# Turning fifteen of sixteen x tiles by transposing loads, and moving the points at which two sets of weights are waited for

## The chip, the core and the metric

The kernel runs on one core of a Trainium2 chip. A core has engines with an instruction queue each: TensorE (PE in the profile; its weight loads are PEld), VectorE (DVE), ScalarE (ACT), GpSimd (POOL) and SyncE (SP), which here issues nearly all DMAs. Each engine runs its instructions in the order of its queue and waits on semaphores. Matrix products go from the on-chip memory (SBUF) into eight banks of a second one (PSUM), from which ScalarE and VectorE evacuate them. The metric is the time on the device in microseconds (us), as a median of several runs.

## The reference, cut to what matters

x has 2048 rows (tokens) of 1024. Two branches are computed from it and mixed by a gate:

```python
g = sigmoid((x * gate_w).sum(-1, keepdims=True))
# a: attention, 32 heads of 32, each token over 8 keys at distances 0, 2, .. 14
qkv = x @ wqkv                       # 1024 x 3072
a = softmax(q . k * scale) v @ wo    # over those 8 keys
# b: a gated MLP whose gate mixes tokens
z = gelu(x @ w_in)                   # 1024 x 3584, halves z1 and z2
z2 = layernorm(z2)
b = (z1 * (w_sp @ z2 + b_sp)) @ w_out
return g * a + (1 - g) * b
```

All inputs and the output are bf16.

## The kernel before

Everything is computed from x transposed. The tile `xT` holds it with the 1024 features on the partitions (8 blocks of 128) and the 2048 tokens along the row. Sixteen tiles of 128 tokens make up x.

**How x is turned.** There are two ways. Tiles 0 to 3 are loaded as they are into `xn` (lines 173 to 177) and turned by TensorE: `xpose` (L221) does eight 128x128 transposes into PSUM, and ScalarE (L228) and VectorE (L230) copy every other one into `xT`. Tiles 4 to 15 are loaded by a DMA that transposes (L179, DMA_TRANSPOSE in the profile) and need nothing else. `first_dma` and `chained` tie these first DMAs to each other, so that SP issues them in the order in which they are written; all later DMAs of SP stand behind them.

**The first products.** `keep_warm` issues matmuls on zeros. A small transpose (L324) and a copy (L325) put the gate's weights into a column of `wvp`, the weights of the first three head groups' v. `vp_tile(i)` (L299) multiplies x tile i with them, eight matmuls of 385 columns; in the first four of these the transposes of the next tile are put between the matmuls (`middle`). Then come q and k of head group 0 (`qk_tile`, L290, eight matmuls of 512 columns each, for 512 tokens), more v tiles, and so on. Products q.k are taken in blocks along the diagonal (`band_blocks`, L338; TensorE L356, evacuated by ScalarE at L364), stored to DRAM (`band_d`) and loaded back as `att_L` in a layout with one token's eight keys side by side. SP issues those stores and loads too.

**The attention on VectorE.** There are eight head groups of four heads. Of each, VectorE takes the maxima and subtracts them (L671 to L674), ScalarE takes the exponential (L662), VectorE sums and normalizes (L683 to L687, L692), multiplies with v (L708, four operations of 128x2048 for each half of a group) and adds up the products (L712, L713, L717).

**Products by Strassen's scheme.** Most large products are done as quads: a 2x2 block product by seven instead of eight block products (`strassen` L438, `chain` L499; the matmuls are at L435). In `chain` a quad has seven steps of four matmuls. After the first, ScalarE copies a bank as the seed of another (L518), after the second it copies a bank to SBUF (L524), and after the third and the fifth VectorE adds that copy to a bank (`plus`, L506). TensorE can go on into a bank only once its reader is done. Two quads run interleaved, step by step. The sums of weights that a quad needs are made by VectorE, four operations (`sums4_steps`, L577).

**What sets the order.** Engines run what is written in the order of writing, and a planner decides while the kernel is being written where VectorE's and ScalarE's side work goes. It keeps a clock for each engine; `advance` (L764) looks at what is due by the time of TensorE's clock (DMAs in `due`, the attention's streams, and a list `fill` of weight sums with the time from which each may be placed) and writes the earliest. Times in it are assumed ones. For the weights of the first z2 product, `load_later` (L988) registers eight loads and, when the planner holds the last for landed at time t, enters the four sums with t + `LATE`, 0.5 us:

```python
        def landed(t):
            land[0] += 1
            if land[0] == KT:
                fill.extend((t + LATE, 1.05, f) for f in wz_sums(p))
```

**The z1 stage.** Seven passes fp = 0 .. 6 (L1200) compute two quads each (`z1_quad`); ScalarE evacuates by gelu (L1168), and each quad's result is stored to DRAM (`store`, `z_d` in the profile). The weights of pass 0 are loaded alone and the others for two passes at a time, in two halves f, into `w1_pairs` (`load_w1`, L841). Those of passes 5 and 6 go where those of passes 1 and 2 were. They are loaded at the end of pass 2. In passes 2 to 4 eight transposing loads of w_sp (`load_raw`, L1109, 512 KB each) are put at given steps (`RAW_AT`, L1199), all on SP.

After these follow the token mixing (from L1577 on, by `strassen`) and the output product (L1468 and others), which the change does not touch.

## Time and profile before

| | |
|---|---|
| median of 9 runs | 655.79 us (654.79 to 657.12) |
| the profiled execution | 657.12 us |
| its span, from the first to the last instruction | 655.3 us |
| busy: TensorE, VectorE, ScalarE | 646.1, 518.6, 299.0 us |
| granted clock of TensorE, mean | 0.997 |
| transposing loads of x: SP busy with one (min / median / max) | 1.307 / 1.308 / 2.339 us |
| the same, issue to landing (min / median / max) | 3.7 / 3.9 / 4.9 us |
| matmuls 128x512 of bf16 in L294, mean | 380 ns (they overlap; one starts each 0.22 us) |

How to read it: times are those of one execution, counted from its first instruction. A row of a timeline has the start, the time from the start of its first to the end of its last instruction, the engine (with a q where it is its sequencer, which waits or issues), the line of the kernel, the operation, what it writes and reads, and how many are merged; in brackets stand the idle time before it and what ended it. A row of the waits has the waiting instruction, what released it, the total, the number and the longest. The granted clock is the share of its full clock that TensorE was given.

### The profile page before, as it was taken

The page shows a single profiled execution, that of the slowest core. Times are in us where ns is not written, and L with a number is a line of the kernel's source. Part 1 is how long each engine was busy: PE and PEld are TensorE (multiplying, and loading weights), DVE is VectorE, ACT ScalarE, POOL GpSimd, SP SyncE. Part 2 cuts the span into 40 slices and gives each one's busy share as a digit, 9 for nine tenths or more (in the row PEclk, how much of TensorE's full clock was granted, in tenths as well). Part 3 has the DMA queues.
Part 4 walks back from the last instruction along what each step waited for, and adds up shares of the span by engine and source line. Part 5 has one row for each costly group of instructions (what it writes and reads, how often), then busy time and mean ns, then how long its engine had stood idle before and what let it go on. Part 6 is the DMA issues. An engine that isn't in the chain of part 4 may idle for free.

```text
span 655.3 us, 11411 instructions
## 1 busy us (share of the span) xinstructions
PE 646.1 (99%) x4425; PEld 339.0 (52%) x4425; DVE 518.6 (79%) x820; ACT 299.0 (46%) x652; POOL 6.2 (1%) x15
## 2 busy tenths in 40 slices
PE   8999999999989999999999999999999999999998
PEld 4544467544445555444444444444444444868684
DVE  2533989999799999999898676977559999596862
ACT  4545677776676787899654112112121112202020
POOL 1000000000000000001000000000000000000000
PEclk9999999999999999999999999999999999999999
DMA  9989555696767104246994578559587375454501
GB/s 219 190 216 233 103 111 150 148 236 160 176 182 209 24 1 125 65 129 186 287 234 152 133 166 176 145 144 279 134 186 173 98 142 100 110 148 107 135 28 54
DMA packets 230198, 98.19 MB, mean 150 GB/s; under 512 B 177520, under 2 KB 217088, under 8 KB 230144
## 3 DMA queue, kind: packets, MB, share of 16 engines
q1 hardware_dynamic: 229856, 97.27, 61.0%
q8 instruction: 34, 0.56, 0.4%
q10 hardware_dynamic: 288, 0.20, 0.1%
q14 instruction: 20, 0.16, 0.1%
HBM read 45.10 MB, written 36.61 MB: 125 GB/s over the span
## 4 chain that ended last, share of the span: by engine, by line
PE 86%; DVE 5%; ACT 4%; DMA 3%; issue 1%; SPq 0%; DVEq 0%; ACTq 0%
PE psum_all L435 67%; PE psum_all L1468 8%; PE psum_all L294 7%; PE psum_all L304 3%; DMA arena<-in_B_w_in_dram 2%; ACT arena L870 1%; DVE arena L708 1%; PE psum_all L356 1%; ACT arena L1168 1%; DVE arena L577 1%; DVE psum_all L506 1%; DMA arena<-in_A_x_dram 1%; DVE arena L712 1%; ACT arena L815 0%; ACT arena L364 0%
## 5 line engine op out<-in xcount | busy, mean ns | idle before, releaser
L435 PE MATMUL psum_all<-arena 128*128 128x512 f16 (+6 forms) x2462 | 494.6, 363 | 3.5 <-DVE psum_all L506 2.4
L435 PEld LDWEIGHTS <-arena 128*128 128x128 f16 (+1 forms) x2462 | 240.1, 98 | 250.5 <-issue 7.2
L708 DVE TENSOR_TENSOR arena<-arena,att_A 128x2048 f16<-128x2048 bf16 x64 | 75.3, 1220 | 0.3
L294 PE MATMUL psum_all<-arena 128*128 128x512 bf16 x256 | 57.5, 380 | 0.0
L506 DVE TENSOR_TENSOR psum_all<-psum_all,arena 128x512 f32<-128x512 f32 (+1 forms) x74 | 48.5, 669 | 8.5 <-PE psum_all L435 4.7
L1468 PE MATMUL psum_all<-arena 128*128 128x256 f16 (+1 forms) x468 | 51.6, 273 | 0.0
L1468 PEld LDWEIGHTS <-arena 128*128 128x128 f16 x468 | 45.8, 98 | 5.5
L815 ACT ACTIVATE arena<-psum_all 128x448 bf16<-128x448 f32 x64 | 34.3, 544 | 20.3 <-PE psum_all L435 9.7
L453 ACT COPY psum_all<-psum_all 128x512 f32<-128x512 f32 (+1 forms) x24 | 12.5, 519 | 67.6 <-PE psum_all L435 66.8
L1168 ACT ACTIVATE arena<-psum_all 128x512 bf16<-128x512 f32 x56 | 31.2, 613 | 20.9 <-PE psum_all L435 8.7
L294 PEld LDWEIGHTS <-arena 128*128 128x128 bf16 x256 | 24.4, 98 | 28.4 <-issue 0.2
L712 DVE TENSOR_TENSOR arena<-arena 128x2048 f16<-128x2048 f16 x32 | 38.1, 1219 | 0.0
L364 ACT CAST arena<-psum_all 128x1988 f16<-128x1988 f32 (+3 forms) x25 | 34.0, 1359 | 2.7 <-PE psum_all L356 2.4
L870 ACT ACTIVATE arena<-arena 128x896 bf16<-128x896 bf16 x32 | 30.9, 979 | 0.0
L577 DVE TENSOR_TENSOR arena<-arena 128x512 f16<-128x512 bf16 (+3 forms) x52 | 25.5, 522 | 6.5 <-DMA arena<-in_B_w_in_dram 6.0
L297 ACT CAST arena<-psum_all 128x512 bf16<-128x512 f32 x32 | 18.6, 585 | 25.8 <-PE psum_all L294 25.8
L477 ACT COPY psum_all<-psum_all 128x512 f32<-128x512 f32 (+1 forms) x24 | 12.4, 518 | 37.5 <-PE psum_all L435 36.8
L581 DVE TENSOR_TENSOR arena<-arena 128x1024 f16<-128x1024 f16 (+2 forms) x17 | 12.2, 722 | 19.1 <-PE psum_all L435 15.7
L464 ACT COPY psum_all<-psum_all 128x512 f32<-128x512 f32 (+1 forms) x24 | 12.4, 517 | 25.8 <-PE psum_all L435 24.8
L459 ACT COPY arena<-psum_all 128x512 f32<-128x512 f32 (+1 forms) x24 | 12.7, 533 | 24.7 <-PE psum_all L435 22.5
L518 ACT COPY psum_all<-psum_all 128x512 f32<-128x512 f32 (+1 forms) x37 | 20.6, 567 | 5.7 <-PE psum_all L435 5.1
L304 PE MATMUL psum_all<-arena 128*128 128x385 bf16 x128 | 22.6, 327 | 0.0
(112 smaller groups left out, 522.3 us busy)
## 6 DMA issues: line engine op xcount, KB each, us to landing
arena<-v_d SPq DMA_DIRECT2D x8, 960.0 KB, 6.5
z_d<-arena SPq DMA_DIRECT2D x14, 512.0 KB, 4.5
arena<-z_d SPq DMA_DIRECT2D x14, 512.0 KB, 4.2
zg_d<-arena SPq DMA_DIRECT2D x56, 128.0 KB, 2.2
arena<-zg_d SPq DMA_DIRECT2D x32, 224.0 KB, 3.3
band_d<-arena SPq DMA_DIRECT2D x28, 248.5 KB, 4.0
arena<-in_A_wqkv_dram SPq DMA_DIRECT2D x16, 256.0 KB, 4.5
o_d<-arena SPq DMA_DIRECT2D x4, 1024.0 KB, 6.1
```

Of the source, the lines that this page charges most:

```text
L294: nc.tensor.matmul(ps[:], w[:, t, kt, :], xT[:, kt, 512 * c:512 * (c + 1)], start=(kt == 0), stop=(kt == KT - 1))
L304: nc.tensor.matmul(ps[:, 0:VP + 1], xT[:, kt, i * P:(i + 1) * P], wvp[:, kt, :], start=(kt == 0), stop=(kt == KT - 1))
L364: nc.scalar.copy(dst, src)
L435: nc.tensor.matmul(bank[:, 0:N], lhsT, rhs, start=(start and m == 0), stop=(m == n - 1), skip_group_check=True)
L506: last_add[0] = nc.vector.tensor_tensor(out[:, n], a[:, n], vs, ALU.add)
L577: return [lambda a=a: nc.vector.tensor_tensor(*a) for a in args]
L708: lambda ws=ws, in0=in0, in1=in1: tt(p5[:, ws], in0[:, ws], in1[:, ws], ALU.mult)), False
L712: lambda a=p3[:, ws], b=p3[:, ws.start + 4:ws.stop + 4]: tt(a, a, b, ALU.add)), not n
L815: nc.scalar.activation(z2[:, i + 8 * a, ZC * c:ZC * (c + 1)], bank[:, 0:ZC], ACT.Gelu_apprx_tanh, accum_out=s1[:, 4 * n + c:4 * n + c + 1])
L870: return nc.scalar.activation(junk, src, ACT.Square, accum_out=(s2, s2h)[x][:, n:n + 1])
L1168: last_gelu[0] = nc.scalar.activation(z1s[:, f, a, :], bank[:], ACT.Gelu_apprx_tanh)
L1468: nc.tensor.matmul(bank[:, h], l, r, start=(start and m == 0), stop=(m == len(ab) - 1), skip_group_check=True)
```

## The change

The diff has four parts.

1. Only x tile 0 is loaded plainly and turned by TensorE. Tiles 1 to 15 are loaded by transposing DMAs. The two loads of group 0's q and k weights stand behind tile 3 in SP's order (before: behind tile 5).
2. Two of the eight warm-up matmuls go, the transposes of tile 0 come ahead of the gate column's transpose, and nothing is put between the matmuls of the first v tiles.
3. The planner's allowance after the last z2 weight load is 4.0 instead of 0.5 us, so the four sums are written later.
4. In pass 2 of the z1 stage the third w_sp transpose moves to pass 3, the first half of the weights of passes 5 and 6 is loaded at step 6 of the pass, the second half at its end, and the two stores of pass 2 are issued behind both.

```diff
@@ -165,6 +165,7 @@
         for t in range(2):
             dma(wqk_slots[g][:, t], wq_v[:, :, t * D + g * C:t * D + (g + 1) * C])
 
+    PLAIN = 1
     nc.scalar.dma_start(gw_s[:], gw_v)
     def load_wvp(k, dma):
         dma(wvp[:, k:k + 2, 0:VP], wq_v[:, k:k + 2, 2 * D:2 * D + VP])
@@ -173,11 +174,9 @@
     first_dma(xn[:, 0:1, :], x_v[:, 0:1, :])
     for k in range(2, KT, 2):
         load_wvp(k, first_dma)
-    for i in range(1, 4):
-        first_dma(xn[:, i:i + 1, :], x_v[:, i:i + 1, :])
-    for i in range(4, 16):
+    for i in range(PLAIN, 16):
         chained(nc.sync.dma_start_transpose(xT[:, :, i * P:(i + 1) * P], x2[i * P:(i + 1) * P, :]))
-        if i == 5:
+        if i == 3:
             load_wqk(0, first_dma)
     load_wqk(1, first_dma)
     first_dma(bass.AP(tensor=v_d.tensor, offset=v_d.offset, ap=[[C, 16], [(S + 16) * C, NG], [1, C]]), zeros)
@@ -320,13 +319,13 @@
             pinned.setdefault(inst.ins.engine, inst.ins.name)
 
     keep_warm(6)
+    xpose(0)
     gwT = banks[1][:, 0:KT // 2].bitcast(BF)
     nc.tensor.transpose(gwT, gw_s[:], ident[0:KT, 0:KT])
     nc.vector.tensor_copy(wvp[:, :, VP:VP + 1], gwT.rearrange("p (k o) -> p k o", o=1))
-    keep_warm(2)
-    xpose(0)
+    pass
     for i in range(4):
-        vp_tile(i, middle=lambda: xpose(i + 1) if i < 3 else None)
+        vp_tile(i, middle=None)
     band_at = [0]
     last_sub = [None]
     last_evac = [None]
@@ -639,7 +638,7 @@
         sync.dma_start(v_t, bass.AP(tensor=v_d.tensor, offset=v_d.offset + (g * (S + 16) + 2) * C, ap=[[NJ * C, P], [1, NJJ * C]]))
 
 
-    FR, LATE = 0.4, 0.5
+    FR, LATE, WZ_LATE = 0.4, 0.5, 4.0
     t_bands, t_v = [FAR] * NG, [FAR] * NG
     sub_end, exp_end = [FAR] * NG, [FAR] * NG
     v_data = [0.0]
@@ -838,8 +837,8 @@
     def w1_half(fp, f):
         return w1_first[:, f] if fp == 0 else w1_pairs[(fp - 1) // 2 % 2][f][:, :, (fp - 1) % 2 * P:((fp - 1) % 2 + 1) * P]
 
-    def load_w1(fp):
-        for f in range(2):
+    def load_w1(fp, halves=(0, 1)):
+        for f in halves:
             to = w1_first[:, f] if fp == 0 else w1_pairs[(fp - 1) // 2 % 2][f]
             sync.dma_start(to, win_v[:, :, HF * f + fp * P:HF * f + (fp + (2 if fp else 1)) * P])
 
@@ -991,7 +990,7 @@
         def landed(t):
             land[0] += 1
             if land[0] == KT:
-                fill.extend((t + LATE, 1.05, f) for f in wz_sums(p))
+                fill.extend((t + WZ_LATE, 1.05, f) for f in wz_sums(p))
         for n, f in enumerate(load_wz(p)):
             dma(at + gap * n, 0.65, f, landed, True)
 
@@ -1141,7 +1140,7 @@
     z1s_slots = [[free(o + 2048 * r, 2048).rearrange("p (f a t) -> p f a t", f=2, a=2) for r in range(2)] for o in (T1_OFF, R_OFF + 16384)]
     zv_slots = [free(R_OFF + 20480 + 1024 * r, 1024, F32) for r in range(2)]
 
-    w1_left = [0]
+    w1_left, kept_stores = [0], []
 
     def w1_sums(fp):
         def one(f):
@@ -1167,7 +1166,10 @@
             act(0.6 + table("gelu"), max(clock["PE"], clock["DVE"] if f + a == 2 else 0.0) + 0.2)
             last_gelu[0] = nc.scalar.activation(z1s[:, f, a, :], bank[:], ACT.Gelu_apprx_tanh)
 
-        def store():
+        def store(now=False):
+            if fp == 2 and not now:
+                kept_stores.append(store)
+                return
             dst = z1_d[c].rearrange("p (f t) -> p f t", f=NF)[:, fp:fp + NFH + 1:NFH, :]
             last_store[0] = sync.dma_start(dst, z1s.rearrange("p f a t -> p f (a t)"))
 
@@ -1196,7 +1198,7 @@
     dma(clock["PE"] + 1.0, 2.9, lambda: load_w1(1), w1_landed(1))
     RAW_IN = 3.0
     DRAIN, SUMS = 1, NFH - 2
-    RAW_AT = {2: {2: 0, 4: 1, 6: 2}, 3: {4: 3, 6: 4}, 4: {2: 5, 4: 6, 6: 7}}
+    RAW_AT = {2: {2: 0, 4: 1}, 3: {2: 2, 4: 3, 6: 4}, 4: {2: 5, 4: 6, 6: 7}}
     for fp in range(NFH):
         while w1_left[0]:
             advance(max(clock["PE"], clock["DVE"]) + 0.5)
@@ -1206,12 +1208,18 @@
             fill.extend((clock["PE"] + RAW_IN, 1.15, f) for f in wsp_sums(0, 0))
         late = () if fp else [b[2] for b in bank_roles]
         at = [0]
-        run(z1_quad(fp, 0), z1_quad(fp, 1), hooks={3: lambda: mark(late, 512, ZC), **{n: lambda a=a: load_raw(0, a) for n, a in RAW_AT.get(fp, {}).items()}},
-            step=lambda: z1_step(fp, at))
+        hooks = {3: lambda: mark(late, 512, ZC), **{n: lambda a=a: load_raw(0, a) for n, a in RAW_AT.get(fp, {}).items()}}
+        if fp == 2:
+            hooks[6] = lambda: load_w1(5, (0,))
+        run(z1_quad(fp, 0), z1_quad(fp, 1), hooks=hooks, step=lambda: z1_step(fp, at))
         if fp == DRAIN:
             drain()
-        if fp in (0, 2):
-            load_w1(fp + 3)
+        if fp == 0:
+            load_w1(3)
+        if fp == 2:
+            load_w1(5, (1,))
+            for f in kept_stores:
+                f(True)
         if fp == NFH - 3:
             load_rows()
     while fill:
```

The order in which the built programs stand shows what moves. TensorE has 26 matmuls fewer, 24 transposes and two warm-ups, and is otherwise the same. On VectorE the first group of z2 sums stands behind one L708, the four operations L671 to L674 and another L708; later in the same stage one L712 falls behind a pair of L506 that it preceded, and of the second set of z2 sums two of four fall behind a pair of L506, while the L713 and L717 that followed them come ahead of the sums. On ScalarE the exponential of group 6 (L662), with the two loads of function tables around it, moves from the first pair of z2 quads to the second; that of group 5 comes one copy sooner. On SP, besides what is said above, both loads of the v weights of groups 3 to 7 follow the stores of v tiles 4 to 7, and the loads of group 2's q and k weights stand further back, behind the bands' stores and one of them behind the v stores of tiles 8 to 11.

## The prediction

> **What bounds the kernel now.** I read the shares of busy time first, then TensorE's busy time in stretches of 10 us, then who waited for whom, and last the timelines of the two stretches in which TensorE is not full.
>
> ```profile
> PE 646.1 (99%) x4425; PEld 339.0 (52%) x4425; DVE 518.6 (79%) x820; ACT 299.0 (46%) x652; POOL 6.2 (1%) x15
> ```
>
> TensorE is busy for 646.1 of 655.3 us. So a change can win only by taking matmuls away, by closing some of 9.2 us of holes, or by removing time at a lower clock. The stretches (start:end, length, TensorE busy and instructions, granted clock, DMA share, GB/s) say where those are:
>
> ```profile
> 0.00:10.00 10.00, 8.16 (x51) 1.00 0.81 243
> ...
> 80.00:90.00 10.00, 9.19 (x155) 1.00 0.39 88
> ...
> 180.00:190.00 10.00, 9.39 (x118) 1.00 0.50 113
> 190.00:200.00 10.00, 7.91 (x34) 0.83 0.98 286
> ...
> 320.00:330.00 10.00, 9.70 (x46) 1.00 1.12 261
> ```
>
> Holes: 1.8 us at the start (1.2 of it before the first matmul), 0.8 at 80 to 90, 0.6 and 2.1 at 180 to 200, 0.3 at 320, and some 3 at the very end. Only the row of 190 has a lower clock. Who ended the waits:
>
> ```profile
> DVE att_m L671 <- DMA att_L<-band_d: 6.7, 1, 6.7
> ...
> DVE arena L577 <- DMA arena<-in_B_w_in_dram: 6.0, 2, 3.4
> ...
> DVE arena L683 <- ACT att_L L662: 3.1, 1, 3.1
> ...
> PE psum_all L435 <- DVE psum_all L506: 2.4, 2, 2.1
> ```
>
> The 3.4 us wait of L577 is that for the z2 weights; its other 2.6 us is for the w1 weights. The 2.1 us of the last row is the hole at 192.3.
>
> **The start.** The queue of SP and the first work of TensorE (start, duration):
>
> ```profile
> 2.69 1.42 SPq L162 DMA_DIRECT2D arena<-in_A_x_dram  x3
> 4.14 3.73 SPq L179 DMA_TRANSPOSE arena<-in_A_x_dram  x2
> 7.92 1.21 SPq L162 DMA_DIRECT2D arena<-in_A_wqkv_dram  x2
> 9.18 15.11 SPq L179 DMA_TRANSPOSE arena<-in_A_x_dram  x10
> ```
>
> Removed from TensorE: the transposes of x tiles 1 to 3, three groups of 8 that took 0.86, 0.91 and 0.91 us = 2.7, and two warm-up matmuls, 0.66. The gate column moves behind the transposes of tile 0. The new path: six warm-ups end at 3.93; transposes of tile 0 0.84, to 4.8; VectorE's four copies (0.79) and then the column's copy (0.19) let the first v tile begin at 5.3 and end at 6.8 (8 matmuls in 1.47). Tile 1 now comes by a transposing load at the place of its plain load, 2.69. The first such load landed 4.8 us after its issue, behind three plain loads; the median of the twelve is 3.9. That gives 6.6 to 7.5, and I take 7.1, between the two. Tiles 2 and 3 follow at the issue's own pace of 1.35 (1.31 and a gap): 8.5 and 9.8. So the fourth v tile runs 9.8 to 11.3. The weights of group 0, issued at 6.8 to 7.8, land 3.9 later, by 12.3 at most for the second half, in time; q and k (3.62) end at 14.9. Before they ended at 16.70. Win there: 1.8, or 1.2 if one of the loads is as slow as the slow ones of before; I take 1.5. Later tiles land each 1.35 to 1.5 us from 13 on and are wanted from 15 on each 1.47, so they are covered by about 1 us.
>
> [...] The row: a transposing load keeps SP 1.31 us at least (2.34 at most), a plain one 0.43. [...] By the row it costs 3 x 1.35 - 1.42 = 2.6 us of SP, and I go by the row. What is queued behind: twelve more tiles, the weights of group 1, the stores of v and of the bands, the other weights, and then the load of group 0's bands. SP issues all of this without a hole above 0.15 us until 55 us, so the delay travels:
>
> ```profile
> 51.65 1.29 SPq L190 DMA_DIRECT2D att_L<-band_d  x2
> 55.47 0.29 DVE L671 TENSOR_TENSOR att_m<-att_L 128x256 f16<-128x256 f16 x1 [6.70 <-DMA att_L<-band_d]
> 59.17 0.63 ACT L662 ACTIVATE att_L<-att_L 128x512 f16<-128x512 f16 x1
> 59.70 0.59 ACT L518 COPY psum_all<-psum_all 128x512 f32<-128x512 f32 x1
> ```
>
> VectorE waits for those bands at L671, its four operations end at 56.70, and the exponential L662 on ScalarE waits for them. Behind it in ScalarE's order stands the seed copy L518, and TensorE's third product of that quad (four matmuls of 0.23 after 59.65, so 60.6) waits for L518. L518 ends 1.12 after the exponential begins; the earliest is 56.8 + 1.1 = 57.9, so there are 2.7 us of slack today. The win is therefore min(1.5, 2.7 - d), d being the delay of the bands. Bounds of d: twelve transposes took 2.7 us more than 12 x 1.35 (three issues of 2.1 to 2.3). If two of these three stretched issues go away, d is 0.8; if one more comes, 3.4. I take 1.8, because the plain loads that crowded the DMA engines ahead of them are gone. Win 0.9; ends -0.7 and 1.5. SP is idle again from 66.2 to 67.7, so nothing is carried to the bands of the next group.
>
> **The z2 weights.** VectorE (start, total, count):
>
> ```profile
> 167.31 1.23 DVE L708 TENSOR_TENSOR arena<-arena,att_A 128x2048 f16<-128x2048 bf16 x1
> 171.94 2.22 DVE L577 TENSOR_TENSOR arena<-arena 128x1792 f16<-128x1792 bf16 x2 [3.41 <-DMA arena<-in_B_w_in_dram]
> 174.07 0.29 DVE L671 TENSOR_TENSOR att_m<-att_L 128x256 f16<-128x256 f16 x1
> ...
> 193.69 1.16 DVE L506 TENSOR_TENSOR psum_all<-psum_all,arena 128x448 f32<-128x448 f32 x2
> ```
>
> The planner now puts one L708, the four maxima L671 to L674 and another L708 ahead of the four sums. But the maxima read bands whose second half is issued at 170.06 and lands 2.4 later, at 172.5. The wait that ended at 171.9 is replaced by one that ends at 172.5. From there: maxima 1.15, L708 1.15, four sums 4.2, L708 1.2: 180.3, against 180.75. The mended wait by itself is worth 0.45.
>
> More comes from the order that follows: the first two additions L506 no longer stand behind an L712 (1.22). They begin at 192.1 instead of 193.69, TensorE restarts at 192.8 instead of 194.36, and the hole shrinks by 1.6. Next, the third addition stands behind two L712 and ends at 196.05: TensorE, now ahead, waits 0.3 there; in the next pair of quads four L708 end at 203.1, 0.2; in the third the maxima and the exponential of group 7 come later, 0.25. Left: 0.85. ScalarE's exponential moves to the second pair; between its last evacuation (199.4) and the addition that needs its copy (203.1) the two table loads and it fit: 0.52 + 1.3 + 0.53 + 0.5 from 199.9 give 202.8. Without that gap of 0.3 each further delay of ScalarE would be TensorE's.
>
> The clock is the other term. The row of 190 has 0.83, and in single microseconds 0.50 from 195.2 to 198.6: 3.4 us at half, a loss of 1.7. [...] The profiled execution, 657.12, is the slowest of nine and 1.3 over their median, which fits. No hole that I foresee is above 0.7, and today's 0.65 at 88 left the clock at 1.00. So the win is 0.85 + 1.7 = 2.5 in an execution like the profiled one and 0.85 in one that keeps its clock. For the median I take the middle, 1.7; ends 0.4 (only the mended wait) and 3.8 (hole and clock whole).
>
> **The w1 weights.** The last pair of half loads is issued behind two w_sp transposes instead of three, ahead of the stores of pass 2. It landed at 321.57; two steps sooner (2.2 and 1.3) it is there before VectorE asks at 319.0. TensorE's hole at 326 goes: 0.3, or 0 if something else fills it. The stores are read only from 350 on, which hides their delay; the third w_sp transpose joins three others of pass 3 and 4, and the last one keeps its place.
>
> **Sum.** 0.9 + 1.7 + 0.3 = 2.9 off the median 655.79: 652.9. Against the profiled execution: 655.3 - 0.9 - 2.5 - 0.3 = 651.6 of span, and 1.8 around it: 653.4.
>
> **The rivals.**
> - SP's delay eats the whole start (d of 2.7), and the z2 wait is only renamed: the maxima's wait in place of the sums', 0.45 left because additions come up against ScalarE's later exponential. With 0.3 for w1: 655.0. For it: the 6.7 us wait of L671 and the bands' 172.5. Against it: the L712 is out of the way of L506 whatever the bands do.
> - SP barely notices (d below 1.2), and the median execution does lose its clock today: 1.5 + 2.5 + 0.3, 651.5. For it: the 0.8 us in which VectorE idles ahead of L506 at 204.6; against it: 1.31 against 0.43.
> - Slower: the stretched issues. They follow each other closely in the first transposing loads. If 8 of 15 last 2.2, the queue is 15 x 1.35 + 8 x 0.85 long and d is 2.6 + 6.8 - 2.7 = 6.7: the third product of group 2's quad starts 4.0 later than before, less 2.0 of the other wins: 657.8. It decides from d = 4.7 on, about five and a half stretched issues. Against it: the last seven of today's twelve show none.
>
> **How the numbers follow.** Chances: forecast 0.5 (its own range 651.8 to 654.4), first rival 0.2, second 0.16, third 0.14. A change under 0.2% (1.3 us) is about what nine runs with this spread cannot tell from none. Faster: 0.5, 0.16 and a few hundredths of the first rival less those of the forecast's end, 0.66; same: most of the first rival, 0.18; slower: the third with its edges, 0.16. The range leaves out half of each outer rival: 650.9 to 656.6.
>
> **What would show it.** Right: first q and k end near 15; L671 of group 0 starts at 56 to 58 and TensorE has a hole of about half a us at 59; a wait of L671 for att_L near 170 in place of L577's; no clock below 1.00 near 195; no hole at 326. Wrong: transposing issues above 2 us in number, a hole above 1.5 us near 60, or L506 still holding TensorE for 2 us near 190.

## The result

The changed kernel takes 652.70 us, the median of 9 runs (651.49 to 653.56). The kernel before, run beside it, takes 655.55 (29 runs), so the ratio is 0.995, with a 95% interval of 0.9938 to 0.9962. The difference of the medians, 2.85 us, is more than twice the 1.3 us below which the prediction would not have told it from no change. On another chip (run `a0_after` below) it was 652.02 against 655.36, a ratio of 0.9944 (0.9926 to 0.9961).

The profiled execution took 652.59 us, its span 650.8. The first part of its page, the busy time of each engine:

```profile
PE 643.0 (99%) x4399; PEld 337.3 (52%) x4399; DVE 515.4 (79%) x808; ACT 295.8 (45%) x640; POOL 6.2 (1%) x15
```

TensorE is busy for 3.1 us less than the 646.1 before. Its stretches of 10 us (TensorE busy and instructions, granted clock, DMA share, GB/s):

```profile
0.00:10.00 10.00, 7.88 (x37) 1.00 0.86 188
...
80.00:90.00 10.00, 9.19 (x157) 1.00 0.41 92
180.00:190.00 10.00, 9.38 (x118) 1.00 0.65 159
190.00:200.00 10.00, 10.00 (x54) 1.00 1.01 272
320.00:330.00 10.00, 10.00 (x48) 1.00 1.06 264
```

The stretches at 190 and 320 have no hole any more, and the clock is whole. Those at 80 and 180 are as before. Who ended VectorE's waits for loads:

```profile
DVE att_m L670 <- DMA att_L<-band_d: 9.9, 2, 7.8
...
DVE arena L576 <- DMA arena<-in_A_wqkv_dram: 2.0, 1, 2.0
```

The wait for the z2 weights (L577 before) has left the list. The wait for bands is there twice in place of once: 7.8 us for group 0's, and 2.1 for those of group 5 at 171. The second row is new, for group 2's q and k weights; TensorE has no hole behind it.

Both traces can be laid over each other, since after the first v tiles TensorE does the same matmuls in the same order. Lining them up from the end gives TensorE's lead, the time by which one product starts sooner than in the profile of before:

| at | lead, us | what changed it |
|---|---|---|
| 16 (end of the first q and k) | 0.81 | the start |
| 60.3 | 0.24 | a hole of 0.41 behind L517 |
| 191 to 194 | 2.50 | the hole of 2.09 is gone |
| 198.7 | 4.18 | no half clock |
| 326 | 4.64 | the hole of 0.30 is gone |
| the end | 4.5 | |

So of 4.5 us in span, 0.24 come from the start, 2.26 from the z2 stage, 1.7 from the clock and 0.46 from w1 (some 0.1 is lost again behind). Without the clock it is 2.8, close to the difference of the medians. The first rows at which the start is read, SP's queue:

```profile
2.69 5.29 SPq L178 DMA_TRANSPOSE arena<-in_A_x_dram  x3
8.02 1.21 SPq L162 DMA_DIRECT2D arena<-in_A_wqkv_dram  x2
9.27 18.36 SPq L178 DMA_TRANSPOSE arena<-in_A_x_dram  x12
```

Three issues took 5.29 us instead of 3 x 1.35: 1.62, 2.27 and 1.31. And the stretch near 60, SP, VectorE, ScalarE and TensorE in order of time:

```profile
54.04 1.29 SPq L189 DMA_DIRECT2D att_L<-band_d  x2
57.85 0.29 DVE L670 TENSOR_TENSOR att_m<-att_L 128x256 f16<-128x256 f16 x1 [7.79 <-DMA att_L<-band_d]
59.12 0.63 ACT L661 ACTIVATE att_L<-att_L 128x512 f16<-128x512 f16 x1 [0.66 <-DVE att_L L673]
59.66 0.58 ACT L517 COPY psum_all<-psum_all 128x512 f32<-128x512 f32 x1
60.29 1.02 PE L434 MATMUL psum_all<-arena 128*128 128x512 f16 x4 [0.41 <-ACT psum_all L517]
```

The bands landed 2.38 us later than before (57.75, 55.37). The exponential waited for them, the seed copy stood behind the exponential, and TensorE waited for the seed copy. In the z2 stage VectorE reads:

```profile
171.40 0.29 DVE L670 TENSOR_TENSOR att_m<-att_L 128x256 f16<-128x256 f16 x1 [2.14 <-DMA att_L<-band_d]
...
173.69 4.22 DVE L576 TENSOR_TENSOR arena<-arena 128x1792 f16<-128x1792 bf16 x4
...
190.87 1.16 DVE L505 TENSOR_TENSOR psum_all<-psum_all,arena 128x448 f32<-128x448 f32 x2
191.94 2.35 DVE L711 TENSOR_TENSOR arena<-arena 128x2048 f16<-128x2048 f16 x2
```

The wait has changed its name from weights to bands, and the additions L505 come 2.8 us sooner than in the profile before, ahead of both L711.

### The profile page after: what moved, and what is told of

Its sections match the earlier page's. It is cut to its first block, busy times and chain, and to the rows that moved or that the text cites. A ratio compares the mean times of both kernels' runs of the same rounds, so it can differ in the third digit from the quotient of the medians.

```text
span 650.8 us, 11331 instructions
## 1 busy us (share of the span) xinstructions
PE 643.0 (99%) x4399; PEld 337.3 (52%) x4399; DVE 515.4 (79%) x808; ACT 295.8 (45%) x640; POOL 6.2 (1%) x15
## 4 chain that ended last, share of the span: by engine, by line
PE 90%; ACT 4%; DVE 2%; SPq 1%; DMA 1%; issue 1%; ACTq 0%; DVEq 0%
PE psum_all L434 70%; PE psum_all L1476 8%; PE psum_all L293 8%; PE psum_all L303 2%; ACT arena L869 1%; PE psum_all L355 1%; ACT arena L1167 1%; SPq L178 1%; PE psum_all L821 1%; DMA arena<-in_A_wqkv_dram 1%; ACT arena L363 1%; ACT arena L814 1%; DVE psum_all L505 1%; DMA att_L<-band_d 0%; SPq L189 0%
## 5 line engine op out<-in xcount | busy, mean ns | idle before, releaser
L505 DVE TENSOR_TENSOR psum_all<-psum_all,arena 128x512 f32<-128x512 f32 (+1 forms) x74 | 48.4, 669 | 7.8 <-PE psum_all L434 3.9
L452 ACT COPY psum_all<-psum_all 128x512 f32<-128x512 f32 (+1 forms) x24 | 12.5, 520 | 66.9 <-PE psum_all L434 66.2
L711 DVE TENSOR_TENSOR arena<-arena 128x2048 f16<-128x2048 f16 x32 | 38.0, 1218 | 0.0
L296 ACT CAST arena<-psum_all 128x512 bf16<-128x512 f32 x32 | 18.7, 585 | 28.2 <-PE psum_all L293 28.2
L476 ACT COPY psum_all<-psum_all 128x512 f32<-128x512 f32 (+1 forms) x24 | 12.3, 518 | 37.4 <-PE psum_all L434 36.8
L417 DVE TENSOR_TENSOR arena<-arena 128x2048 f16<-128x2048 bf16 x8 | 9.4, 1222 | 20.0 <-DMA arena<-in_A_x_dram 19.9
L463 ACT COPY psum_all<-psum_all 128x512 f32<-128x512 f32 (+1 forms) x24 | 12.4, 517 | 25.6 <-PE psum_all L434 24.8
```

What stands on the lines that cost most here:

```text
L505: last_add[0] = nc.vector.tensor_tensor(out[:, n], a[:, n], vs, ALU.add)
L711: lambda a=p3[:, ws], b=p3[:, ws.start + 4:ws.stop + 4]: tt(a, a, b, ALU.add)), not n
```

## The experiments

There are twelve runs, in four groups on three chips: `e1` to `e4`; `a0`, `e2b`, `e7` and `e8`; `e5`, `e9` and `e10`; `e12`. Kernels of one group share a chip and the runs of the kernel before. The first and third group had the same chip, on which the kernel before took 659.32 and 658.84; on the second group's it took 655.36, on the fourth's 657.66. Loads take longer in one profile than in another: one of the z2 weight loads took 6.1 us from issue to landing in the changed kernel (160.09 to 166.18) and 8.1 in `e2_z2` (162.16 to 170.25), between 6.9 and 8.1 in three profiles of the first group and between 6.4 and 7.6 in three of the second.

### One part alone

Parts 1 and 2 (the start):

```diff
-    for i in range(1, 4):
-        first_dma(xn[:, i:i + 1, :], x_v[:, i:i + 1, :])
-    for i in range(4, 16):
+    for i in range(1, 16):
...
-        if i == 5:
+        if i == 3:
...
+    xpose(0)
...
-    keep_warm(2)
-    xpose(0)
...
-        vp_tile(i, middle=lambda: xpose(i + 1) if i < 3 else None)
+        vp_tile(i, middle=None)
```

> The kernel before with parts 1 and 2 of the change alone (x tiles 1 to 3 by transposing loads, the order of the start); w1 and z2 as before. My theory: the start wins about 0.8 us on TensorE, the later bands of group 0 take all but 0.2 to 0.3 of it near 60 us, and the z2 hole of about 2 us near 193 stays, so the time is within 0.5 us of the kernel before (655.0 to 655.5). Rival, the start is where the gain comes from and keeps it: 654.0 or less. In the profile: VectorE's wait of group 0's bands ends near 57.8 instead of 55.4, a hole of about 0.4 near 60.

660.08 us, ratio 1.0014 (0.9989 to 1.0039). The bands landed at 57.90, 2.53 late; TensorE had a hole of 1.17 before 60.43, behind which its lead was 0.09. So next to nothing was left of the start against the first profile of before, as my theory said, and the rival's 654.0, a ratio of 0.9976, lies outside the interval, which still allows a gain of 0.7. One caution: in that profile of before the bands landed sooner than in any other with the old start. Two of those ran on the chip of `e1_start`, and behind 60 they stand 0.94 (`e2_z2`) and 0.23 (`e3_w1`) behind the profile of before, so `e1_start` is ahead of both. The z2 hole stayed, 2.27.

Part 3 (z2), run in the first group and again beside the changed kernel in the second:

```diff
-    FR, LATE = 0.4, 0.5
+    FR, LATE, WZ_LATE = 0.4, 0.5, 4.0
...
-                fill.extend((t + LATE, 1.05, f) for f in wz_sums(p))
+                fill.extend((t + WZ_LATE, 1.05, f) for f in wz_sums(p))
```

> The kernel before with part 3 alone (allowance after the last z2 weight load 4.0 instead of 0.5). My theory: this is most of the whole gain. The wait of VectorE for the z2 weights is replaced by one for the bands that ends about as late, but the first two additions to PSUM no longer stand behind a sum of products of 1.2 us, so the hole of 2 us near 193 is gone: 2.1 to 2.3 us less, 653.4; where the half clock near 196 is gone too, up to 3.9 less. Rival, the wait is only renamed: 0.5 us less, 655.1.

658.29 us, ratio 0.9991 (0.9973 to 1.0009): at most 1.8 us, where I had expected 2.1 to 2.3. The profile had a hole of 2.48 us near 196. VectorE waited until 175.55 for the bands, much longer than in the changed kernel.

> Part 3 alone once more, beside the changed kernel. My theory: the hole near 193 has the length (time of the bands' landing + 19.5 of VectorE's work + 0.7) less the time at which TensorE gets there, as in the first run of it (175.5 + 20.1 = 195.6 against 193.6); with the same bands as in the changed kernel of this call, relative to TensorE, its hole is the changed kernel's plus or less the difference of TensorE's lead. Rival, the parts need each other: hole of 2 us in this kernel, none in the changed kernel, with bands that land alike.

654.24 us, ratio 0.9986 (0.9976 to 0.9997), so 0.9 us gained. The profiled execution, 656.57, was one of the slower of 21 (653.02 to 658.24). VectorE and TensorE in it:

```profile
175.24 0.30 DVE L671 TENSOR_TENSOR att_m<-att_L 128x256 f16<-128x256 f16 x1 [4.81 <-DMA att_L<-band_d]
...
194.71 1.16 DVE L506 TENSOR_TENSOR psum_all<-psum_all,arena 128x448 f32<-128x448 f32 x2
195.39 1.86 PE L435 MATMUL psum_all<-arena 128*128 128x448 f16 x9 [2.09 <-DVE psum_all L506]
```

The order of VectorE is the new one (L506 ahead of both L712), and the hole is as long as in the kernel before. In this stage the changed kernel has the same order; there the bands landed at 171.30, here at 175.15. A hole set by the bands fits this; that the order removes the hole by itself does not.

Part 4 (w1):

```diff
-    RAW_AT = {2: {2: 0, 4: 1, 6: 2}, 3: {4: 3, 6: 4}, 4: {2: 5, 4: 6, 6: 7}}
+    RAW_AT = {2: {2: 0, 4: 1}, 3: {2: 2, 4: 3, 6: 4}, 4: {2: 5, 4: 6, 6: 7}}
...
+        if fp == 2:
+            hooks[6] = lambda: load_w1(5, (0,))
...
+        if fp == 2:
+            load_w1(5, (1,))
+            for f in kept_stores:
+                f(True)
```

> The kernel before with part 4 alone (order of the loads in pass 2 of the z1 stage). My theory: the hole of 0.3 us near 326 goes and nothing else, 0.3 to 0.45 us less, 655.2. Rival, another load (w_sp) comes late in its place: no gain.

657.93 us, ratio 0.9983 (0.9969 to 0.9997): 1.1 us, more than I had expected. On this chip the hole that part 4 closes was 1.96 (in the start's profile, first row below) and 1.81 (in that of part 3), against 0.30 in the first profile of before; in the two of the second group without part 4 it was 0.49 (`e7_wz2`) and none (`e2b_z2`). In the first three TensorE starts again 4.72 us after VectorE's wait for these weights ends (326.32 - 321.60 before, 326.38 - 321.66, 329.42 - 324.70). With part 4 there is none. But a new one came, here in TensorE's row (the second):

```profile
326.38 4.87 PE L432 MATMUL psum_all<-arena 128*128 128x512 f16 x14 [1.96 <-DVE psum_all L503]
...
353.15 3.18 PE L436 MATMUL psum_all<-arena 128*128 128x512 f16 x13 [0.70 <-DVE psum_all L507]
```

Of the nine profiles of kernels with part 4, those of the changed kernel (two) and of `e8_wqk1` show no hole there, five others 0.35 to 0.81, and one 0.09. Of the five without it, none does. In one (`e9_pool`) VectorE waits for a load some 15 us before it:

```profile
336.93 1.23 DVE L1125 TENSOR_TENSOR arena<-arena 128x2048 f16<-128x2048 bf16 x1 [1.66 <-DMA arena<-in_B_w_sp_dram]
```

It waits there for the last of the eight w_sp loads, issued at 330.74; the other seven had landed by 333.48, the third, which part 4 puts off, at 319.36. So part 4, which I had taken for free, can cost up to 0.8; that it does so by the load that it moves is not shown.

### The changed kernel again, and half of part 3

> The changed kernel unedited, on the chip on which the next three run. The runs with parts 1, 2 and 3 alone have changed my theory: part 3 renames the wait, and whether the hole near 193 goes is decided by when the last bands of its group land. With them at 171.3, as in the first profile of the changed kernel, no hole; 1 us later some 0.5 us of hole, 2 us later 1.5. So: where its loads land as in that profile, 2.5 to 3 us faster than before; where they land 3 us later, about 1 us or less. Rival, the new order removes the hole by itself: 2.5 us or more faster everywhere, no hole near 193 wherever the bands land.

652.02 us, ratio 0.9944 (0.9926 to 0.9961). The bands of group 5 let VectorE go on at 171.31 and TensorE has no hole above 0.11 there, as my theory says for bands as early as that; the rival fits this run as well, and fails at part 3 alone. Near 60, VectorE and TensorE:

```profile
57.47 0.29 DVE L670 TENSOR_TENSOR att_m<-att_L 128x256 f16<-128x256 f16 x1 [8.18 <-DMA att_L<-band_d]
...
59.91 1.02 PE L434 MATMUL psum_all<-arena 128*128 128x512 f16 x4 [0.90 <-ACT psum_all L517]
```

Here the start had won 1.68 (tile 1 landed at 6.92, where it was 7.78 in the first profile), the bands were 2.01 late, and 0.62 was left.

```diff
-    FR, LATE, WZ_LATE = 0.4, 0.5, 4.0
+    FR, LATE, WZ_LATE = 0.4, 0.5, 2.0
```

(the second line is this kernel, the first that of part 3 alone)

> Part 3 alone with an allowance of 2.0 instead of 4.0: one sum of products (L708) and one weight sum stand ahead of the maxima that wait for the bands, three weight sums behind, and the L712 of 1.2 us stays ahead of the first two additions L506. My theory, both moves count alike: of the 2.3 us of VectorE's work that part 3 takes out of the stretch from the wait to the additions, only the L708 goes here, so the hole is about 1.2 us longer than in part 3 alone. Rival, only the wait matters: hole as in part 3 alone. Rival, only the L712 matters: hole as in the kernel before.

654.26 us, ratio 0.998 (0.9969 to 0.9991), and no hole near 193. VectorE:

```profile
171.39 1.09 DVE L577 TENSOR_TENSOR arena<-arena 128x1792 f16<-128x1792 bf16 x1 [1.59 <-DMA arena<-in_B_w_in_dram]
172.40 0.28 DVE L671 TENSOR_TENSOR att_m<-att_L 128x256 f16<-128x256 f16 x1
...
191.88 1.16 DVE L506 TENSOR_TENSOR psum_all<-psum_all,arena 128x448 f32<-128x448 f32 x2
```

I had expected 1.2 us more of a hole than with part 3 alone, and had less. As to the path I was right: TensorE could go on at 192.56, 21.17 us after the wait, which lies between 22.42 for the old order and 20.15 for the new. As to the wait I was wrong: it was for the weights again, and these came at 171.4; the bands, 0.9 later, found VectorE busy with the first sum. So the L712 need not move for the hole to go; what counts is the end of the wait plus the length of the path. Of the 2.1 us of the hole, 1.25 are the shorter path (22.42 - 21.17), and 0.85 come from weights that landed earlier by TensorE's time (171.94 - 171.39, and TensorE is 0.30 later). TensorE got there at about the same time, 192.57.

### What sets the hole at 193

The row of TensorE in the profile of before, with the hole:

```profile
194.36 5.82 PE L435 MATMUL psum_all<-arena 128*128 128x448 f16 x21 [2.09 <-DVE psum_all L506]
```

The profiles together. The wait is the last one of VectorE ahead of the sums, given by the start of the instruction behind it:

| kernel | waits for | its end | TensorE restarts | difference | hole |
|---|---|---|---|---|---|
| before | weights | 171.94 | 194.36 | 22.42 | 2.09 |
| start alone | weights | 172.04 | 194.46 | 22.42 | 2.27 |
| w1 alone | weights | 172.41 | 194.84 | 22.43 | 2.33 |
| part 3 alone, first | bands | 175.55 | 196.08 | 20.53 | 2.48 |
| part 3 alone, again | bands | 175.24 | 195.39 | 20.15 | 2.09 |
| `e4_act` | bands | 179.85 | 200.00 | 20.15 | 1.96 |
| `e5_more` | bands | 181.27 | 201.43 | 20.16 | 1.96 |
| `e9_pool` | bands | 173.00 | 193.15 | 20.15 | 0.28 |
| `e12_swap` | bands | 172.25 | 192.39 | 20.14 | 0.25 |
| changed | bands | 171.40 | 191.54 at the earliest | | none |

The path is as long as the order makes it, to 0.02 us (the first run of part 3 alone has another wait of 0.31 in it). Part 3 takes 2.27 off it: one L708 and one L712. But it hangs it on the bands, which came 1.2 to 2.7 us later than the weights in the four profiles of the changed kernel and of part 3 alone (171.30 and 169.88, 171.22 and 170.00, 175.45 and 173.84, 175.15 and 172.49). By this count the net is between a gain of 1.1 and a loss of 0.4. So the order alone does not make the 2.26 us of the first profile. An estimate from the table and the landings: with the old order, weights at 169.88 would have let TensorE go on at 169.88 + 0.18 + 22.42 = 192.5, where it arrived at 192.0; in the second profile of the changed kernel the same sum gives 192.6 against 191.7. Holes of 0.5 and 0.9 would have been left in place of 2.09. The rest of the hole went because in these two profiles weights and bands both landed earlier than in the profile of before.

To see it as a cause, I made the bands late in the changed kernel:

```diff
     def load_bands(g):
...
-        for e in range(2):
+        for e in (0, 1, 1) if g == 5 else (0, 1):
```

> The changed kernel, with the second half of group 5's bands loaded twice, the second load waiting for the first (work without use). The order of TensorE, VectorE and ScalarE is the same. The bands for which VectorE waits near 171 land about 2.5 us later. My theory (the new order of the z2 sums takes away the hole near 193 only while the bands land before about 172): a hole of 1.8 to 2.4 us near 193, about 2 us slower than the changed kernel, a ratio to before of about 0.998, and more where the clock falls. Rival, the new order removes the hole by itself: no hole near 193, as the changed kernel.

659.14 us, ratio 1.0011 (0.9996 to 1.0026). The changed kernel itself has no run on this chip; against its ratio of 0.9944 to 0.995 elsewhere this is some 4 us more, where I had expected 2, but against `e9_pool`, the nearest kernel on the same chip (657.80), it is 1.3. VectorE, ScalarE and TensorE:

```profile
179.85 0.29 DVE L670 TENSOR_TENSOR att_m<-att_L 128x256 f16<-128x256 f16 x1 [6.24 <-DMA att_L<-band_d]
181.12 0.63 ACT L661 ACTIVATE att_L<-att_L 128x512 f16<-128x512 f16 x1 [6.53 <-DVE att_L L673]
181.66 2.03 ACT L296 CAST arena<-psum_all 128x512 bf16<-128x512 f32 x4
182.28 2.02 PE L821 MATMUL psum_all<-arena 128*128 128x448 bf16 x5 [2.60 <-ACT arena L296]
...
200.00 1.29 PE L434 MATMUL psum_all<-arena 128*128 128x448 f16 x6 [1.54 <-DVE psum_all L505]
```

The hole is back, 1.54, where the path says that it must be: 200.00 - 179.85 is again 20.15. The edit accounts for only a part of the delay. The second half of the bands landed first at 176.63, already 5.3 us later than in the changed kernel, and the repeated load at 179.75; this execution, 662.21, was also one of the slower of 22 (657.33 to 663.73). A second hole shows what I had not seen: the exponential of these bands stands in ScalarE's order ahead of the copies of q and k (L296), so TensorE waited 2.60 for those first. This is the chain of 60 us once more. (The same profile has a hole of 2.20 at 84.8, behind bands of group 1 that came late; the edit does not touch those.)

### What eats the start

First the delay made longer. The added loads are done again later, where they were:

```diff
-    load_wqk(1, first_dma)
+    [load_wqk(g, first_dma) for g in (1, 2, 3)]
```

> The changed kernel, with four more loads of 256 KB on SP behind tile 15: the q and k weights of groups 2 and 3, which are loaded again later where they were, so these loads are work without use. The order of TensorE, VectorE and ScalarE is the same. SP reaches group 0's bands about 2.5 us later than in the changed kernel, so 4.5 to 4.9 later than before. My theory, win at 60 us = min(lead of the start, 2.7 - delay): TensorE is 1.8 to 2.2 us behind the kernel before after a hole of 2.6 to 3.9 us near 60, and the kernel is about 2.4 us slower than the changed kernel, 4.1 if the clock falls there: a ratio to before of 0.998 to 1.001. Rival, SP's delay is hidden: as the changed kernel, 0.995.

661.47 us, ratio 1.0048 (1.003 to 1.0067); the rival, a hidden delay, is out. SP, VectorE and TensorE:

```profile
27.28 7.66 SPq L162 DMA_DIRECT2D arena<-in_A_wqkv_dram  x6
59.54 1.28 SPq L189 DMA_DIRECT2D att_L<-band_d  x2
63.53 0.29 DVE L670 TENSOR_TENSOR att_m<-att_L 128x256 f16<-128x256 f16 x1 [7.48 <-DMA att_L<-band_d]
65.97 1.87 PE L434 MATMUL psum_all<-arena 128*128 128x512 f16 x4 [6.79 <-ACT psum_all L517]
```

The bands landed at 63.44, 8.07 late, and TensorE was 5.45 behind: 2.7 - 8.07 is -5.37. The mechanism holds over the whole range, but I had the delay wrong: four loads cost 5.7 to 6.1 us more than in the two profiles of the changed kernel, not 2.5. The issues themselves became longer: the six of the first row took 7.66 us, where the two of the changed kernel took 1.21. The added 1.05 MB at that pace is 173 to 184 GB/s, a little under what the stretches from 10 to 50 us carry (182 to 233 GB/s in the changed kernel). That fits a queue which is paced here by bytes and not by a fixed time of an issue; no run separates the two.

The formula against the profiles with the new start in which the bands, and nothing else, could hold TensorE at 60:

| kernel | lead of the start | bands late by | 2.7 less that | lead behind 60 |
|---|---|---|---|---|
| changed | 0.81 | 2.38 | 0.32 | 0.24 |
| changed, again | 1.68 | 2.01 | 0.69 | 0.62 |
| start alone | 1.43 | 2.53 | 0.17 | 0.09 |
| `e10_bands` | 1.29 | 1.92 | 0.78 | 0.70 |
| `e5_more` | 1.51 | 8.07 | -5.37 | -5.45 |

With a slack of 2.62 in place of 2.7 it is exact to 0.02. It holds for the old start too: in `e2_z2` the bands came 3.57 late, and TensorE stood 0.94 behind. So bands also come late where the start was not touched: in the five profiles with the old start they landed between 55.37 (before, the earliest) and 58.94. How much of the 2.0 to 2.4 in the changed kernel is due to the change therefore stays open.

Then three attempts to take the delay away. The first two move weight loads to ScalarE's queue, at the start (all four) or behind x tile 3 (those of group 1):

```diff
-        if i == 3:
-            load_wqk(0, first_dma)
-    load_wqk(1, first_dma)
+    load_wqk(0, nc.scalar.dma_start)
+    load_wqk(1, nc.scalar.dma_start)
```

> The changed kernel, with the four loads of the q and k weights of groups 0 and 1 issued by ScalarE at the start instead of by SP. SP then issues four DMAs fewer (about 2.5 us) ahead of group 0's bands. My theory (SP's delay of those bands is what ate the start's gain): the bands are issued 2 us or more sooner than in the changed kernel, the hole of 0.4 us near 60 is gone, TensorE keeps its whole lead of the start (0.8, or 1.1 if its wait for group 0's weights goes as well): 0.6 to 0.9 us faster than the changed kernel, about 652.0. Rival (the bands don't hold TensorE there, or the early weights delay the first x tiles by as much): no faster than the changed kernel, 652.7 or more.

```diff
-    load_wqk(1, first_dma)
...
+    load_wqk(1, lambda o, i: tc.add_manual_dep(nc.scalar.dma_start(o, i).ins, last_gl[0].ins.name, NOSYNC, reason="behind tile 3"))
```

> The changed kernel, with the two loads of group 1's q and k weights issued by ScalarE behind its copies of x tile 3 instead of by SP behind tile 15. The order of TensorE's and VectorE's work is the same. SP issues two DMAs (about 1.2 us) fewer ahead of group 0's bands. My theory: the bands land about 1.2 us sooner than in the changed kernel, the hole of 0.4 us near 60 is gone, and TensorE keeps the lead of the start, 0.4 to 0.6 us faster than the changed kernel. Rival, the bands don't hold TensorE near 60 or something else comes late in their place: as fast as the changed kernel.

662.22 us, ratio 1.0053 (1.0031 to 1.0074), and 658.55, 1.0044 (1.0027 to 1.0062). Both are slower than before, for a reason that neither theory had. ScalarE's first rows in `e4_act`, and then ScalarE's and TensorE's in `e8_wqk1`:

```profile
1.80 6.89 ACTq L166 DMA_DIRECT2D arena<-in_A_wqkv_dram  x4
8.73 1.28 ACT L226 ACT_TABLE_LOAD   x1 [8.73 <-issue]
```

```profile
14.94 5.54 ACTq L328 DMA_DIRECT2D arena<-in_A_wqkv_dram  x2
20.53 1.07 ACT L296 CAST arena<-psum_all 128x512 bf16<-128x512 f32 x2 [8.89 <-DMA arena<-in_A_x_dram]
...
21.65 0.35 PE L355 MATMUL psum_all<-arena 32*64 32x64 bf16 x16 [5.23 <-ACT arena L296]
```

The issue ahead of these four in `e4_act` took 0.41 us (L171, at 1.36); the four took 6.89, and the two of `e8_wqk1` 5.54. The second of the two went out at 20.08, right behind the landing of an x tile at 20.06, which I read as a wait for that landing. ScalarE's own work came only behind the issues, the table load at 8.73 in the one and a cast at 20.53 in the other. TensorE lost 5.78 us at 10 and 5.23 at 21. So they say nothing on the bands; they show what an issue can cost on an engine that also computes.

The third uses GpSimd, which in the changed kernel is busy for 6.2 of 650.8 us, and from 2.7 to 302 not at all:

```diff
-    load_wqk(1, first_dma)
+    load_wqk(1, nc.gpsimd.dma_start)
```

> The changed kernel, with the two loads of group 1's q and k weights issued by GpSimd, which has nothing else to do, instead of by SP behind tile 15. (Issued by ScalarE they held its copies, since an issue waits for the landing of an earlier DMA; an idle engine can wait.) The order of TensorE, VectorE and ScalarE is the same as in the changed kernel. My theory: the bands of group 0 land 1.2 us sooner than in the changed kernel, the hole near 60 (0.4 and 0.9 us in its two profiles) is gone or below 0.2, TensorE keeps the lead of the start: 0.5 to 0.9 us faster than the changed kernel, a ratio to before of about 0.9935. Rival, the loads crowd x tiles at the start or something else comes late at 60: no faster than the changed kernel.

657.80 us, ratio 0.9985 (0.997 to 0.9999). The rival was right. Its TensorE:

```profile
9.23 1.48 PE L303 MATMUL psum_all<-arena 128*128 128x385 bf16 x8 [1.64 <-DMA arena<-in_A_x_dram]
```

The two loads went out at 2.63 and 3.69, and x tile 1 landed at 9.19. The lead of the start was -0.60, and so there was nothing for the bands (2.57 late) to eat. With the same 512 KB behind the x tiles on SP's queue, in the two profiles of the changed kernel, tile 1 had landed at 7.78 and 6.92. So moving them to another queue did not keep them out of the way of x here.

The last run leaves the loads as they are and takes TensorE's dependence on the bands away:

```diff
-            events += [(sub_end[g] + LATE, 1, g) for g in range(NG) if sub_end[g] < FAR and not hold[0]]
+            events += [(sub_end[g] + LATE + 0.6 * (g == 0), 1, g) for g in range(NG) if sub_end[g] < FAR and not hold[0]]
```

> The changed kernel, with the time at which the planner may place the exponential of group 0 0.6 us later. ScalarE then makes the seed copy (L517) before that exponential instead of behind it; VectorE's weight sums and additions of the next 15 us are interleaved a little differently; TensorE's and SP's order is the same. The bands land as late as in the changed kernel. My theory (TensorE is held near 60 only because its seed copy stands behind an exponential that waits for the bands): the hole of 0.4 to 0.9 us near 60 is gone though the bands are as late, TensorE keeps most of the lead of the start past 62, and the kernel is 0.3 to 0.8 us faster than the changed kernel, a ratio to before of about 0.9935 on a chip like the first two, more on one whose DMAs are slow. Rival, the hole only moves to the next copy or addition (L523, L505), which still stand behind the exponential: a hole of the same size at 61 to 63.

653.01 us against 657.66, ratio 0.9927 (0.9904 to 0.995). ScalarE and TensorE:

```profile
57.81 0.57 ACT L517 COPY psum_all<-psum_all 128x512 f32<-128x512 f32 x1 [0.33 <-PE psum_all L434]
58.29 0.63 ACT L661 ACTIVATE att_L<-att_L 128x512 f16<-128x512 f16 x1
...
64.12 2.75 PE L434 MATMUL psum_all<-arena 128*128 128x512 f16 x12 [0.39 <-DVE psum_all L505]
...
83.18 1.02 PE L434 MATMUL psum_all<-arena 128*128 128x512 f16 x4 [0.84 <-DVE psum_all L505]
```

The seed copy is ahead of the exponential and there is no hole at 60: the lead of 1.80 from the start was still 1.67 at 61.5. The bands landed at 56.91, 1.54 late and so less late than in the changed kernel, but by the formula that would have left 1.1. So the exponential in ScalarE's order is the cause. But the lead does not last. VectorE's addition at 63.4 stood behind a weight sum that waited 0.62 for its load, and the one at 82.4 behind the bands of group 1; the lead was 0 at 83.2. The rival is right in its kind, though not in the place. This is the lowest ratio of all kernels, but its interval covers that of the changed kernel, and the profile shows no gain from the swap that reached the end. I don't claim one.

## Why the prediction was right

**As a whole.** 652.9 was predicted and 652.7 measured. The steps of the sum were right in kind, and their sizes were off in both directions: 0.9 for the start, 1.7 for z2 with the clock, 0.3 for w1 against 0.24, 2.26 and 0.46 in the profile, which with the clock left out add up to 2.96, close to the 2.85 of the medians. That the total agrees to 0.2 us is in part luck: the start gave less than forecast, half the clock was counted and not there, and z2 made up for both with loads that happened to land early.

The parts alone do not add up to the whole. Their ratios, 1.0014 (start), 0.9986 (z2, second run) and 0.9983 (w1), come to 0.9983, some 1.1 us, against 0.9944 and 0.995 for all of them together. With the three intervals combined the sum could lie between 0.995 and 1.001, so the gap is at the edge of what the runs can tell. Early landings in the z2 stage of the changed kernel would explain it; that is not shown.

**The start, min(1.5, 2.7 - d).** The formula was right to 0.1. The term d was mis-sized: 1.8, against 2.38 and 2.01 in the two profiles of the changed kernel. (The bounds of d rest on stretched issues: in the profile of before the last six of twelve show none, not the last seven; in the changed kernel four of fifteen were stretched in the first profile, and SP was done with the x tiles 3.3 us later than before, 27.63 against 24.29, of which it had regained 1.0 by the bands.) The 1.5 was 0.81 in the first, where two of the first three issues were stretched, and 1.68 in the second. I had counted SP's time of issue and then taken something off it because fewer plain loads would crowd the engines, which no run shows. The bytes might have told me better. In the first 10 us, 243 GB/s before have become 188, and the 0.55 MB that are missing need 2.8 us at the 197 GB/s of the next stretch; that is an argument from the two profiles, not an experiment. The row of 1.31 us an issue gave 2.6 us of SP's time, against 2.38 and 2.01 by which the bands were late. The slower rival needed d of 4.7; `e5_more` shows that this place would indeed have turned the result.

**z2, 0.85 and the clock.** "A wait replaced by one that ends at 172.5, worth 0.45", and L506 no longer behind an L712: both right, and the table above has them as one path that is 2.27 shorter. Two sizes were off. The bands came at 171.3, by TensorE's time about 1 us sooner than before, so the hole went altogether and not by 1.6; that was luck as far as the runs show, since in both runs of part 3 alone the bands came at 175 and the hole stayed. And of the later stalls, 0.75 in my sum, none came in the first profile and 0.27 in the second. Whether that early landing belongs to the change stays open. Shifted by TensorE's lead at 181, the bands landed between 171.4 and 172.8 in six profiles with the new start and at 174.0 in two (`e4_act`, `e5_more`; `e10_bands`, where the edit bears on them, is left out); in the five without it, the one of before among them, between 172.0 and 174.6.

**The clock.** In an execution like the profiled one 1.7 were won, as predicted. For the median I had added half of it, my estimate between an execution that loses its clock and one that keeps it, and that half was not there. 657.12 less 1.7 is 655.4, the median of before; and beside the changed kernel on the second chip, 39 of 43 executions of the kernel before list a mean clock of 1.000 (median 655.29) and 3 list 0.997 (658.43). So the median execution kept its clock there, and most likely on the chip of the result too, where only the profiled execution of before has a clock on record. The 0.85 that was missing from this term was made up by the hole that closed further than predicted.

**w1, 0.3.** 0.46, for the reason given. That the moved loads cost nothing held in the profiles of the changed kernel; elsewhere part 4 came with a new hole of up to 0.8, and the hole that it closes was between none and 2.

**The first rival**, SP's delay eats the start and z2 is only renamed, is a fair account of part 3 alone and of the start alone. It was not the changed kernel's, whose bands came in time. **The second**, 651.5, had SP's delay below 1.2, which no profile of the change shows.

## What to carry to other kernels

When a wait is taken away by reordering, write down what the path hangs on afterwards, and compare the two landing times: the gain is the path's shortening less the difference of the landings, and the second term moved from one execution to the next (1.2 to 2.7 us in four profiles of the same order). When DMAs are changed at the head of a queue that is never idle, count bytes against the measured GB/s of the stretch as well as issue times (here four loads cost 5.7 us and more, not 2.5), and follow the delay to the first transfer that something waits for. In these runs an instruction that waited for a late transfer held what stood behind it in its engine's order (near 60 us the exponential held the seed copy, and TensorE had a hole of 0.41 and 0.90 in the changed kernel; with the copy ahead of it, in `e12_swap`, there was none), so look there before trying to make the transfer earlier.

## What the runs showed of the hardware

- A plain load of 256 KB kept SP's sequencer 0.4 us (x, L162 in the profile of before) to 0.6 (q and k weights, the two from 8.02 in the changed kernel). In `e5_more` six took 7.66 us from 27.28, and each of the four added ones made the bands 1.4 to 1.5 us later.
- The second issue on ScalarE's queue in `e8_wqk1` went out at 20.08, 5.1 us after the first and 0.02 after the landing of an x tile, and ScalarE's next instruction of its own began at 20.53.
- The clock of TensorE. In `e5_more` the idle time began at 59.18. The windows of 1 us (TensorE busy, clock, DMA share, GB/s) show when the clock fell and came back:

```profile
62.00:63.00 1.00, 0.00 (x0) 1.00 1.13 157
63.00:64.00 1.00, 0.00 (x0) 0.64 0.99 294
64.00:65.00 1.00, 0.00 (x0) 0.50 0.86 276
...
69.00:70.00 1.00, 1.00 (x4) 0.50 0.92 353
70.00:71.00 1.00, 1.00 (x6) 0.95 0.99 340
```

  It was at half from 63.3 to 70.1, 6.8 us or twice the 3.4 in the profile of before, and all 10 executions of that kernel list a mean clock of 0.994 or 0.995. With holes of 2 us it differs from case to case: in `e1_start` one of 2.27 before 194.46 left the clock at 1.00, and one of 1.96 before 326.38 was followed by half clock from 327.2 to 330.6. On the chip of the first group 26 of 52 executions of the kernel before list 0.997 (median 659.94) and 18 list 1.000 (657.49). The 15 executions of the changed kernel that list a clock have 0.999 or 1.000.
